# Output stores held until the next row's copy is stored, and the transposes of q and k moved in the DMA queue of an attention and MLP kernel

## The chip, the cores and the metric

The kernel runs on one core of a Trainium2 chip. The metric is the device time of one execution in microseconds (us); three runs of the kernel before gave 308.64, 310.31 and 312.22, so its median is 310.31. A core has five engines that run beside each other, each through its own queue of instructions in order: PE (matmuls), DVE (vector operations), ACT (activations and copies), POOL (casts, and the issue of some loads) and SP (the issue of the other DMA transfers). Which engine does what, and in which order, is written out by hand in this kernel; semaphores alone hold one engine back for another.

## What is computed

The reference is an attention with two kinds of masks, followed by a two-layer perceptron with a squared ReLU:

```python
# q, k, v: 8 batches, 8 heads, 576 positions, 64 wide
scores = scale * np.matmul(q, k.transpose(0, 1, 3, 2))
rel = pos[:, None] - pos[None, :]
mask_plain = (rel >= 0) & (rel < 32)                          # heads 0 to 3
mask_dil = (rel >= 0) & (rel < 32 * 4) & (rel % 4 == 0)       # heads 4 to 7
attn = softmax(where(mask, scores, -1e9))
y = np.matmul(attn, v)                # heads side by side: x is 4608 x 512
h = x @ w_in                          # 512 x 2048
g = np.maximum(h, 0.0) ** 2
out = g @ w_out                       # 2048 x 512, float32
```

## The kernel before, in words

**Two streams on PE.** The attention is done batch by batch; a "row" b is one batch, 0 to 7. The perceptron is done in nine blocks c of 512 tokens. Since 576 is more than 512, block c is complete once row c is, and in row b the kernel computes the attention of batch b while the matmuls of block b - 1 fill in between. The block is a Python generator (`moe_gen`), and `pump(n)` takes n steps of it; so the places of the `pump` calls in `attn_scores` and `attn_values` fix the order of PE's instructions. A step of the first layer (`mm1_gen`) is two matmuls, or four where the block's tokens lie on both sides of the end of the ring `xT`; 32 steps make its 16 groups. Each group is squared by ACT (`rt`, L321) and DVE (`g`, L322). From block 2 on, the second layer is a Strassen-like scheme (`mm2_strassen_gen`): DVE makes sums of quarters of g (L331, L332, L406, L418), PE accumulates products in the banks pa, pb and pc, and ACT copies pa out (`take`, L391) before PE adds the next product to the same bank.

**The attention of a row.** Scores are matmuls of the transposed q and k: `QKTp` for the sliding heads (ps, L573) and `QKTd` for the dilated ones (pz, L592). ACT takes the exponential (L563) and DVE multiplies by the mask (L564). The value products are pav (sliding, L622, three pairs of query blocks) and paw (dilated, L638, four). DVE normalises each (reciprocal L605, multiply L610). Then the result is transposed into `xT`: in rows 0 to 3 on PE (px L651, py L669) with a copy by ACT; from row 4 on by a DMA transpose on SP, straight into `xT` for the sliding heads (L680) and through a buffer yd for the dilated ones (L687), which ACT copies into `xT` (L675).

**How the next row is fetched.** From row 2 on, POOL first waits until the transposes into QKTd of this row have landed (`after_transposes`, L235), then loads sliding q and k of the next row (ns, L112) and copies the dilated ones inside DRAM (dd, L207). Somewhere in the row DVE brings ns into token order (nr, L120); SP stores that to DRAM (dp, L217), and later reads it back transposed into QKTp (L225), and dd into QKTd (L229). SP loads v as float32 (sv L132 for sliding, sd L137 for dilated heads); POOL casts it to vp (L169) and vd (L177). The last 32 keys of each query block of vp belong to the next block too, and 64 of vd: these "halos" are copied by ACT (L184, L189) in rows 0 to 2, and by DMA on SP (L194, L197) from row 3 on.

**What sets the order on SP.** SP carries out its list in order; an entry that has to wait (for data, for a buffer, or for the cast on POOL) holds everything behind it. In row 4 to 6 the list before is: vp halo and vd halo of the row; then, from hooks in `attn_values_by_dma`, dp (after the second pav), the two xT transposes, the first yd, sv, the second yd, two QKTp, two QKTd, and sd; then the two stores of the block's results (L397). In rows 2 and 3 one hook, `turn_and_load`, issues dp, sv, sd, two QKTp and two QKTd together. In row 2 it is called after the third pav, in row 3 after the last pz.

**The results.** Blocks 0 and 1 leave as rows of tokens (`store`), blocks 2 to 8 as two halves, ou and ov (`leave`), from a pool of three buffers tagged `ot`. Each store is issued on SP as soon as its half is named complete; only the second half of block 0 is held (`leave_first`).

The lines that the change and the prediction touch are `attn_scores` L692, `attn_values` L706, `attn_values_by_dma` L737, the driver loops L842 to L899, and the helpers named above. The halo rule of `attn_scores` and the hook of row 4 and later read:

```python
            if g and b < 3:
                halo_sliding(b, 0)
...
            av_sliding(b, mp, xs)
            if mp == 1:
                then[0]()
            pump(3)
```

Of the kernel before, what the change touches and what calls it, by code (L numbers as in the profile page):

```python
# [17 lines left out]
def kernel(  # L18
# [174 lines left out]
    def halo_sliding_by_dma(b):  # L193
        nc.sync.dma_start(out=vp[b % 2][0:PADP, 1:NB], in_=vp[b % 2][P - PADP : P, 0 : NB - 1])  # L194
# [29 lines left out]
        for i in (1, 0):  # L224
            nc.sync.dma_start_transpose(out=QKTp[b % 2][:, i, :, PADP:], in_=dp[i])  # L225

    def transpose_dilated(b, dd):
        for i in (1, 0):
            nc.sync.dma_start_transpose(out=QKTd[b % 2][:, i, :, KPAD:], in_=dd[i])  # L229


# [56 lines left out]
    for t, w in zip(wi, wi_cols):  # L288
        r = t.rearrange("p d (g f s) -> p d g f s", f=P, s=4)
        wi4 += [r[:, :, g] for g in range(w // 512)]  # L290

    def mm1_half(c, ffc, ph, dmks):
        lo = c * TOKC % XW
# [59 lines left out]
    def mm2_strassen_gen(c, g):  # L353
        A, Bk, Ck = "abc"
        banks = {}

        def wq(r, q):
            return lambda k: wo[2 * r + k // 4][:, k % 4, HM * q : HM * (q + 1)]

        def gq(i, r):  # L360
            return lambda k, t: g[:, HF * r + k, HTOK * i + P * t : HTOK * i + P * (t + 1)]

        def tq(n):
            return lambda k: wt[n][:, k]

        def sq(n):
            return lambda k, t: gs[n][:, k, P * t : P * (t + 1)]

        def product(bank, a, b, ts=(0, 1)):
            new = bank not in banks  # L370
            if new:
                banks[bank] = pmool.tile([P, 2, HM], FP32, name=f"p{bank}{c}", tag="pm")
            for t in ts:
                for k in range(HF):
                    nc.tensor.matmul(  # L375
                        banks[bank][:, t],
                        a(k, t),
                        b(k),
                        start=(new and t == 0 and k == 0),
                        stop=(k == HF - 1),  # L380
                        skip_group_check=True,
                    )
                    if k % 4 == 3 and (t, k) != (ts[-1], HF - 1):
                        yield

        def half(i):
            return otp.tile([P, 2, DM], FP32, name=f"o{i}_{c}", tag="ot")

        def take(o, j):
            ot = o[:, :, HM * j : HM * (j + 1)]  # L390
            nc.scalar.copy(ot, banks[A])  # L391
            return ot

        def leave(o, i, js):
            t0 = c * TOKC + HTOK * i
            m = slice(HM * js[0], HM * (js[-1] + 1))
            nc.sync.dma_start(  # L397
                out=out[t0 : t0 + HTOK, m].rearrange("(t p) m -> p t m", p=P), in_=o[:, :, m]
            )

        def add(ot, bank):
            nc.vector.tensor_add(ot, banks[bank], ot)  # L402

        last = c == NTOKC - 1

        nc.vector.tensor_sub(g[:, 0:HF, HTOK:], g[:, 0:HF, 0:HTOK], g[:, 0:HF, HTOK:])  # L406
        yield from product(A, gq(0, 0), wq(0, 0))
        upper = half("u")
        o11 = take(upper, 0)
        yield  # L410
        yield from product(Ck, gq(0, 1), wq(1, 0), (0,))
        yield
        yield from product(A, sq(1), tq(1))
        lower = half("v")
        o21 = take(lower, 0)
        yield
        yield from product(Bk, gq(1, 0), tq(2))
        nc.vector.tensor_sub(gs[1], g[:, HF:, 0:HTOK], gs[1])  # L418
        yield
        yield from product(A, sq(0), tq(0))  # L420
        o22 = take(lower, 1)
        add(o22, Bk)
        if last:
            leave(lower, 1, (1,))
        yield
        yield from product(Ck, gq(0, 1), wq(1, 0), (1,))
        add(o11, Ck)
        if last:
            leave(upper, 0, (0,))
        yield  # L430
        yield from product(A, sq(1), wq(1, 1))
        take(upper, 1)
        leave(upper, 0, (1,) if last else (0, 1))
        yield
        yield from product(Bk, gq(1, 1), tq(3))
        add(o21, Bk)
        leave(lower, 1, (0,) if last else (0, 1))
        yield
# [8 lines left out]
        )  # L447

    halves = {}
    first_out = []  # L450

    def leave_first():
        t, o = first_out.pop()
        nc.sync.dma_start(
            out=out[t * P : (t + 2) * P, :].rearrange("(t p) m -> p t m", p=P), in_=o
        )

    def store(c, t, po):
        if t % 2 == 0:
            halves[c] = otp.tile([P, 2, DM], FP32, name=f"ot{c}_{t}", tag="ot")  # L460
        ot = halves[c][:, t % 2]
        nc.scalar.copy(ot, po)
        if c:
            nc.sync.dma_start(out=out[(c * 4 + t) * P : (c * 4 + t + 1) * P, :], in_=ot)
        elif t % 2:
            first_out.append((t - 1, halves[c]))
            if t == 1:
                leave_first()

    def mm2_gen(c, g):  # L470
        for t in range(TOKC // P):
# [220 lines left out]
    def attn_scores(b, gap, less=0, hooks={}):  # L692
        for hp in range(2):
            s_sliding(b, hp)
            if hp in hooks:
                hooks[hp]()
            pump(gap)
        for g in range(2):
            s_dilated(b, g)
            if 2 + g in hooks:  # L700
                hooks[2 + g]()
            if g and b < 3:
                halo_sliding(b, 0)
            pump(gap - less)

    def attn_values(b, gap, wide=False, then=None):  # L706
        xs = x_tiles(b)
        for mp in range(3):
            av_sliding(b, mp, xs)
            if b < 3:  # L710
                if mp < 2:
                    halo_sliding(b, mp + 1)
                else:
                    halo_dilated(b, 0)
            if then and b == 2 and mp == 2:
                then()
            pump(gap)
        x_sliding(b, 0, xs, wide)
        if b < 3:
            halo_dilated(b, 2)  # L720
        pump(gap)
        av_dilated(b, 0, 0, xs)
        if then and b == 1:
            then()
        pump(gap)
        x_sliding(b, 1, xs, wide)
        pump(gap)
        av_dilated(b, 0, 1, xs)
        pump(gap)
        for a in range(2):  # L730
            av_dilated(b, 1, a, xs)
            pump(gap)
        x_dilated(b, 0, xs, wide)
        pump(gap)
        x_dilated(b, 1, xs, wide)

    def attn_values_by_dma(b, then):  # L737
        xs = x_tiles(b)
        for mp in range(3):
            av_sliding(b, mp, xs)  # L740
            if mp == 1:
                then[0]()
            pump(3)
        x_sliding_by_dma(b, xs)
        ys = []
        for t in range(2):
            for a in range(2):
                av_dilated(b, t, a, xs)
                pump(4 + 2 * (a > t))
            ys.append(x_dilated_by_dma(b, t, xs))  # L750
            then[1 + t](ys[t])
        pump(6)
        x_from(b, 0, ys[0])
        pump(7)
        x_from(b, 1, ys[1])
# [70 lines left out]
    for a in range(2):  # L826
        t_dilated(1, m, a, True)
        pump(2)
    attn_scores(1, 2, 1)
    dp = []  # L830
    attn_values(1, 1, True, lambda: dp.append(keep_sliding_qk(2, by_token(2, ns))))
    pump(1000)
    transpose_sliding(2, dp[0])
    transpose_dilated(2, dd)
    leave_first()
    load_v(2)


# [3 lines left out]
    for b in range(2, 4):  # L842
# [5 lines left out]
            cast_v(b)  # L848
        dd = keep_dilated_qk(nxt)
        if b == 3:  # L850
            halo_sliding_by_dma(b)
            halo_dilated_by_dma(b)

        def turn_and_load():
            dp = turn(nxt, ns)
            load_sliding_v(nxt)
            load_dilated_v(nxt, nc.sync)
            transpose_sliding(nxt, dp)
            transpose_dilated(nxt, dd)
            cast_v(nxt)  # L860

        pump(22 if b == 2 else 12)
        attn_scores(b, 4, 0, {3: turn_and_load} if b == 3 else {})
        attn_values(b, b, False, turn_and_load)
        pump(1000)

    for b in range(4, B):
        pending.append(moe_gen(b - 1))
        nxt = b + 1
        if nxt < B:  # L870
            after_transposes(b)
            ns = load_sliding_qk(nxt)
            dd = keep_dilated_qk(nxt)
        if b > 4:
            cast_dilated_v(b)
        halo_sliding_by_dma(b)
        halo_dilated_by_dma(b)
        dps = []

        def copied():  # L880
            if nxt < B:
                dps.append(turn(nxt, ns))

        def first(y):
            if nxt < B:
                load_sliding_v(nxt)

        def second(y):
            if nxt < B:
                transpose_sliding(nxt, dps[0])  # L890
                transpose_dilated(nxt, dd)
                load_dilated_v(nxt, nc.sync)
                nc.gpsimd.tensor_copy(seen, y[:, 0, 0, 0:1])
                cast_sliding_v(nxt)

        pump(3)
        attn_scores(b, 3)
        attn_values_by_dma(b, (copied, first, second))
        pump(1000)  # L899
    pending.append(moe_gen(B - 1))  # L900
    pending.append(moe_gen(B))
# [31 lines left out]
```

## Time and profile before

| what | value |
|---|---|
| median of three runs | 310.31 us |
| the profiled execution: its own time | 309.19 us |
| its span, first to last instruction | 307.1 us |
| granted TensorE clock | 1.00 |
| PE idle, 0 to 25 us / 25 to 277 us / 277 us to the end | 9.9 / 6.8 / 3.9 us |
| SP, DMA packets of its queue (q1) | 68832, 32.96 MB |
| POOL, DMA packets of its queue (q0) | 8752, 13.63 MB |
| longest waits of SP for an engine | 21.8 us (ov, L397), 22.5 us (ou, L397), 17.4 us (dp, L217) |

The profile is one execution on the chip, recorded by the hardware. A timeline line reads: start, length, engine, line of the code, operation, output<-input, and how many instructions are merged. A DMA line on SP or POOL is the time that the issue takes on that queue; the transfer lands later. A line of the waits reads: engine, line and tile that waited <- whom it waited for: total us, times, longest. Over the span, in 40 slices, the DMA engines were busy (in tenths) and moved GB/s:

```profile
DMA  7899998799599999995799979997983231003004
GB/s 116 187 204 213 208 173 152 157 215 221 119 211 176 242 191 187 258 187 120 127 171 260 220 126 188 267 189 131 158 252 22 45 111 40 2 1 139 0 1 138
```

### The profile page before, as it was taken

How to read it: one execution, taken by the hardware profiler on the slowest of the kernel's cores; microseconds unless marked ns; L12 is line 12 of the kernel's file. 1: busy time of each engine (PE TensorE's matmuls, PEld its weight loads, DVE VectorE, ACT ScalarE, POOL GpSimd, SP SyncE). 2: the span in 40 equal slices, each digit the busy share in tenths (PEclk: the TensorE clock that was granted, in tenths of full speed). 3: DMA queues.
4: the chain of work that ended last, by engine and by line, in shares of the span. 5: the costliest groups of instructions: out<-in, count | busy, mean ns of one | idle time of the engine just before them, and what ended most of it. 6: DMA issues, size and time to landing. Idle time of an engine off the chain costs nothing.

```text
span 307.1 us, 6899 instructions
## 1 busy us (share of the span) xinstructions
PE 286.5 (93%) x2762; PEld 192.4 (63%) x2762; DVE 210.1 (68%) x434; ACT 172.9 (56%) x293; POOL 64.2 (21%) x112
## 2 busy tenths in 40 slices
PE   1788998999999899999998999799989999999994
PEld 1345554555554468656887987458745875785584
DVE  7684447758843798489759984999398934834652
ACT  2766648668745863595457636763486446425620
POOL 4481027002704503310027002700230000000000
PEclk9999999999999999999999999999999999999999
DMA  7899998799599999995799979997983231003004
GB/s 116 187 204 213 208 173 152 157 215 221 119 211 176 242 191 187 258 187 120 127 171 260 220 126 188 267 189 131 158 252 22 45 111 40 2 1 139 0 1 138
DMA packets 77616, 47.03 MB, mean 153 GB/s; under 512 B 58480, under 2 KB 69232, under 8 KB 77584
## 3 DMA queue, kind: packets, MB, share of 16 engines
q1 hardware_dynamic: 68832, 32.96, 51.9%
q0 software_dynamic: 8752, 13.63, 26.1%
q8 instruction: 21, 0.34, 0.5%
q14 instruction: 11, 0.09, 0.1%
HBM read 36.70 MB, written 16.52 MB: 173 GB/s over the span
## 4 chain that ended last, share of the span: by engine, by line
PE 72%; DMA 12%; DVE 6%; SPq 3%; ACT 3%; issue 2%; POOL 0%; DVEq 0%; POOLq 0%
PE ph L298 32%; PE pa L375 15%; PE pb L375 7%; DMA vp<-vp 6%; PE po L441 6%; DMA QKTp<-dp 4%; PE pc L375 4%; PE paw L638 2%; PE pav L622 2%; DMA QKTd<-dd 1%; PE ps L573 1%; DMA sv<-in_v_dram 1%; ACT AT L563 1%; SPq L137 1%; SPq L132 1%
## 5 line engine op out<-in xcount | busy, mean ns | idle before, releaser
L298 PE MATMUL ph<-xT,wi 128*128 128x512 f16 (+1 forms) x640 | 134.2, 359 | 0.7 <-ACT xT L675 0.7
L321 ACT ACTIVATE rt<-ph 128x512 f16<-128x512 f32 x144 | 86.2, 608 | 47.5 <-PE ph L298 46.4
L298 PEld LDWEIGHTS <-wi 128*128 128x128 f16 x640 | 68.2, 114 | 45.9 <-issue 0.6
L322 DVE TENSOR_TENSOR g<-rt 128x512 f16<-128x512 f16 x144 | 63.4, 450 | 39.6 <-ACT rt L321 38.1
L375 PEld LDWEIGHTS <-g 128*128 128x128 f16 x448 | 43.3, 98 | 6.1
L375 PEld LDWEIGHTS <-gs 128*128 128x128 f16 x336 | 32.1, 98 | 4.0 <-DVE gs L332 0.3
L441 PE MATMUL po<-wo,g 128*128 128x512 f16 x128 | 33.1, 379 | 0.0
L402 DVE TENSOR_TENSOR ov<-pb,ov 128x512 f32<-128x512 f32 x14 | 9.7, 691 | 30.8 <-PE pb L375 17.4
L375 PE MATMUL pa<-wt,gs 128*128 128x256 f16 x224 | 27.2, 273 | 0.0
L375 PE MATMUL pb<-wt,g 128*128 128x256 f16 x224 | 27.1, 273 | 0.0
L169 POOL CAST vp<-sv 128x512 f16<-128x512 f32 x24 | 15.2, 664 | 53.4 <-DMA sv<-in_v_dram 39.5
L391 ACT COPY ov<-pa 128x512 f32<-128x512 f32 x14 | 8.2, 586 | 30.7 <-PE pa L375 30.7
L177 POOL CAST vd<-sd 128x512 f16<-128x512 f32 (+1 forms) x32 | 22.1, 717 | 11.4 <-PE ph L298 8.0
L610 DVE TENSOR_TENSOR xd<-paw,rcp_d 80x512 f16<-80x512 f32 (+1 forms) x32 | 21.9, 685 | 1.1
L563 ACT ACTIVATE AT<-pz 128x576 f16<-128x576 f32 x32 | 19.7, 694 | 1.2 <-PE pz L592 1.1
L563 ACT ACTIVATE AT<-ps 128x576 f16<-128x576 f32 x32 | 19.2, 657 | 2.2 <-PE ps L573 1.8
L564 DVE TENSOR_TENSOR AT<-AT,maskd 128x576 f16<-128x576 f16 x32 | 18.4, 604 | 1.8 <-ACT AT L563 0.7
L564 DVE TENSOR_TENSOR AT<-AT,maskp 128x576 f16<-128x576 f16 x32 | 15.5, 492 | 5.9 <-ACT AT L563 4.2
L391 ACT COPY ou<-pa 128x512 f32<-128x512 f32 x14 | 8.2, 586 | 15.8 <-PE pa L375 15.7
L610 DVE TENSOR_TENSOR xs<-pav,rcp_p 96x512 f16<-96x512 f32 x24 | 16.5, 687 | 0.8
L622 PEld LDWEIGHTS <-AT 128*128 128x128 f16 x192 | 9.3, 98 | 10.8 <-issue 6.0
L441 PEld LDWEIGHTS <-g 128*128 128x128 f16 x128 | 10.4, 98 | 8.3
(80 smaller groups left out, 276.7 us busy)
## 6 DMA issues: line engine op xcount, KB each, us to landing
sv<-in_v_dram SPq DMA_DIRECT2D x14, 288.0 KB, 5.3
dp<-nr SPq DMA_DIRECT2D x12, 288.0 KB, 4.0
out_dram<-ou SPq DMA_DIRECT2D x6, 512.0 KB, 4.0
out_dram<-ov SPq DMA_DIRECT2D x6, 512.0 KB, 4.7
sd<-in_v_dram SPq DMA_DIRECT2D x8, 320.0 KB, 6.2
ns<-in_k_dram POOLq DMA_DIRECT2D x8, 288.0 KB, 6.3
ns<-in_q_dram POOLq DMA_DIRECT2D x8, 288.0 KB, 7.8
sd<-in_v_dram SPq DMA_DIRECT2D x8, 256.0 KB, 6.0
```

The lines of the kernel that those rows point to most:

```text
L169: nc.gpsimd.tensor_copy(vp[b % 2][:, m : m + 2, :, 0:D], sv[:, :, m : m + 2, :].rearrange("p h m d -> p m h d"))
L177: nc.gpsimd.tensor_copy(vd[b % 2][p0:P, t, c : c + 2, :, 0:D], sd[p0:P, t, :, D * c : D * (c + 2)].rearrange("p h (c d) -> p c h d", d=D),)
L298: nc.tensor.matmul(ph[:, t0:t1], wi4[ffc // 4][:, dmk, :, ffc % 4], xT[:, dmk, x0 : x0 + t1 - t0], start=(dmk == 0 and t0 == 0), stop=(dmk ...
L321: nc.scalar.activation(rt, ph[:], ACTF.Relu)
L322: nc.vector.tensor_mul(g[:, ffc, :], rt, rt)
L375: nc.tensor.matmul(banks[bank][:, t], a(k, t), b(k), start=(new and t == 0 and k == 0), stop=(k == HF - 1), skip_group_check=True,)
L391: nc.scalar.copy(ot, banks[A])
L441: nc.tensor.matmul(po, g[:, ffc, t * P : (t + 1) * P], wo[ffc // 4][:, ffc % 4, :], start=(ffc == 0), stop=(ffc == NFF - 1),)
L563: nc.scalar.activation(AT[:, u, 0:UW], ps[:, :, 0 : UW // 2], ACTF.Exp, scale=scale)
L564: nc.vector.tensor_mul(AT[:, u, 0:UW], AT[:, u, 0:UW], mask)
L610: nc.vector.tensor_tensor(out=x, in0=pv, in1=rb, op=ALU.mult)
L622: nc.tensor.matmul(pav[:, i, h * (D + 2) : h * (D + 2) + D + 1], AT[:, 2 * (h // 2) + m // 3, off : off + P], vp[b % 2][:, m, h, 0 : D + 1 ...
```

## The change

The change makes five edits. (a) `leave_half` takes the place of the store calls; it puts the stores of blocks 2 to 4, and of the second halves of blocks 0 and 1, on a list, and `leave_held` issues the list. The two half-stores of block 1 (256 KB each) become one of 512 KB per pair. (b) In rows 2 and 3, `turn_and_load` runs after the second pav. It issues dp, the held stores, sv, two QKTp, one QKTd, the vp halo of the next row, the other QKTd, and sd; POOL casts sliding v there, and dilated v at the start of the next row. Row 3 pumps 14 steps ahead of the scores where it pumped 12. (c) From row 4 on, `copied` issues dp, the held stores, two QKTp and sv in one go: in row 4 after the second pav, in rows 5 and 6 after the last pz. (d) `loaded` follows the second yd transpose: it casts sliding v, then issues two QKTd, the vp halo of the next row, and sd. (e) In row 1 the first vp halo copy of ACT is put right after the second ps.

```diff
-    def transpose_dilated(b, dd):
-        for i in (1, 0):
+    def transpose_dilated(b, dd, sides=(1, 0)):
+        for i in sides:
             nc.sync.dma_start_transpose(out=QKTd[b % 2][:, i, :, KPAD:], in_=dd[i])
...
+    held = []
+
+    def leave_half(c, i, o, m, hold):
+        def go():
+            t0 = c * TOKC + HTOK * i
+            nc.sync.dma_start(
+                out=out[t0 : t0 + HTOK, m].rearrange("(t p) m -> p t m", p=P), in_=o[:, :, m]
+            )
+
+        if hold:
+            held.append(go)
+        else:
+            go()
+
+    def leave_held():
+        while held:
+            held.pop(0)()
...
         def leave(o, i, js):
...
+            leave_half(c, i, o, slice(HM * js[0], HM * (js[-1] + 1)), 1 < c < 5)
...
-        if c:
-            nc.sync.dma_start(out=out[(c * 4 + t) * P : (c * 4 + t + 1) * P, :], in_=ot)
-        elif t % 2:
-            first_out.append((t - 1, halves[c]))
-            if t == 1:
-                leave_first()
+        if t % 2:
+            leave_half(c, t // 2, halves[c], slice(0, DM), t > 1)
...
-            if g and b < 3:
+            if g and b == 2:
                 halo_sliding(b, 0)
...
-            if then and b == 2 and mp == 2:
+            if then and b > 1 and mp == 1:
                 then()
...
-    def attn_values_by_dma(b, then):
+    def attn_values_by_dma(b, copied, loaded):
...
-            if mp == 1:
-                then[0]()
+            if copied and mp == 1:
+                copied()
             pump(3)
...
             ys.append(x_dilated_by_dma(b, t, xs))
-            then[1 + t](ys[t])
+        loaded(ys[1])
         pump(6)
...
-    attn_scores(1, 2, 1)
+    attn_scores(1, 2, 1, {1: lambda: halo_sliding(1, 0)})
...
-    leave_first()
+    leave_held()
     load_v(2)
...
         if b == 3:
-            halo_sliding_by_dma(b)
+            cast_dilated_v(b)
             halo_dilated_by_dma(b)
 
         def turn_and_load():
             dp = turn(nxt, ns)
+            leave_held()
             load_sliding_v(nxt)
+            transpose_sliding(nxt, dp)
+            cast_sliding_v(nxt)
+            transpose_dilated(nxt, dd, (1,))
+            halo_sliding_by_dma(nxt)
+            transpose_dilated(nxt, dd, (0,))
             load_dilated_v(nxt, nc.sync)
-            transpose_sliding(nxt, dp)
-            transpose_dilated(nxt, dd)
-            cast_v(nxt)
-
-        pump(22 if b == 2 else 12)
-        attn_scores(b, 4, 0, {3: turn_and_load} if b == 3 else {})
+
+        pump(22 if b == 2 else 14)
+        attn_scores(b, 4)
         attn_values(b, b, False, turn_and_load)
...
-        if b > 4:
-            cast_dilated_v(b)
-        halo_sliding_by_dma(b)
+        cast_dilated_v(b)
         halo_dilated_by_dma(b)
-        dps = []
 
         def copied():
             if nxt < B:
-                dps.append(turn(nxt, ns))
+                dp = turn(nxt, ns)
+                leave_held()
+                transpose_sliding(nxt, dp)
+                load_sliding_v(nxt)
 
-        def first(y):
-            if nxt < B:
-                load_sliding_v(nxt)
-
-        def second(y):
+        def loaded(y):
             if nxt < B:
-                transpose_sliding(nxt, dps[0])
-                transpose_dilated(nxt, dd)
-                load_dilated_v(nxt, nc.sync)
                 nc.gpsimd.tensor_copy(seen, y[:, 0, 0, 0:1])
                 cast_sliding_v(nxt)
+                transpose_dilated(nxt, dd)
+                halo_sliding_by_dma(nxt)
+                load_dilated_v(nxt, nc.sync)
 
         pump(3)
-        attn_scores(b, 3)
-        attn_values_by_dma(b, (copied, first, second))
+        attn_scores(b, 3, 0, {3: copied} if b > 4 else {})
+        attn_values_by_dma(b, copied if b == 4 else None, loaded)
```

## The prediction

> **What bounds the kernel now.** I read first the busy times, then the waits of PE, then the timelines of the engines behind those waits. "Row b" is batch b, "MoE c" token block c.
>
> ```profile
> PE 286.5 (93%) x2762; PEld 192.4 (63%) x2762; DVE 210.1 (68%) x434; ACT 172.9 (56%) x293; POOL 64.2 (21%) x112
> ```
> PE is the bound: 307.1 of span less 286.5 leaves 20.6 us idle. By stages, 9.9 of it lie before 25 us and 3.8 after 277, where the change has nothing. The change adds or removes no matmul, so it can only move waits. In PE's waits these two are its targets (total, times, longest):
> ```profile
> PE pav L622 <- DMA vp<-vp: 3.8, 3, 1.6
> PE ps L573 <- DMA QKTp<-dp: 1.0, 1, 1.0
> ```
> The first falls in rows 5, 6 and 7 (at 165.8, 197.2 and 228.9 us). SP's timeline for row 5 says why:
> ```profile
> 151.89 2.65 SPq L225 DMA_TRANSPOSE QKTp<-dp  x2
> 154.64 4.24 SPq L229 DMA_TRANSPOSE QKTd<-dd  x2
> 158.93 1.37 SPq L137 DMA_DIRECT2D sd<-in_v_dram  x2
> 160.41 0.54 SPq L397 DMA_DIRECT2D out_dram<-ou  x1
> 161.04 0.42 SPq L397 DMA_DIRECT2D out_dram<-ov  x1
> 161.55 0.72 SPq L194 DMA_DIRECT2D vp<-vp  x1
> ```
> The halo copy vp<-vp (its source was cast by 155.35 on POOL) stands behind loads and two stores, and lands 5.53 us after issue, with PE waiting. In row 3 QKTp likewise stood behind sv and sd (issues 85.84 to 92.4) and landed at 100.86.
>
> Two places have room for a new wait. In row 3 DVE was busy 8.70 of 8.90 us from 108.3 to 117.2; its end:
> ```profile
> 113.55 0.69 DVE L610 TENSOR_TENSOR xs<-pav,rcp_p 96x512 f16<-96x512 f32 x1
> 114.16 0.41 DVE L322 TENSOR_TENSOR g<-rt 128x512 f16<-128x512 f16 x1
> 114.61 0.69 DVE L331 TENSOR_TENSOR gs<-g 128x1024 f16<-128x1024 f16 x1
> 115.33 0.69 DVE L332 TENSOR_TENSOR gs<-gs,g 128x1024 f16<-128x1024 f16 x1
> 115.94 1.22 DVE L406 TENSOR_TENSOR g<-g 128x2048 f16<-128x2048 f16 x1
> ```
> And row 4 on SP, ACT and PE, in that order:
> ```profile
> 140.03 1.14 SPq L217 DMA_DIRECT2D dp<-nr  x2
> 141.25 3.78 SPq L680 DMA_TRANSPOSE xT<-xs  x2
> 145.66 1.81 SPq L687 DMA_TRANSPOSE yd<-xd  x1
> ...
> 149.99 1.30 ACT L675 COPY xT<-yd 128x640 f16<-128x640 f16 x1
> 152.88 0.59 ACT L391 COPY ov<-pa 128x512 f32<-128x512 f32 x1 [1.58 <-PE pa L375]
> ...
> 153.55 1.91 PE L375 MATMUL pa<-wo,gs 128*128 128x256 f16 x16
> ```
> ACT reads yd at 149.99, then copies bank A out (L391); PE writes that bank again at 153.55. So yd may land at 153.55 - 0.59 - 1.30 = 151.7 at the latest.
>
> **What the Trainium skill says.** "DMA: Bandwidth & Descriptors", Anatomy of one DMA: semaphore waits happen on the issuing sequencer, before dispatch; so a waiting transfer holds all behind it on SP. The trace agrees (the halo above). Same page, "Two DMAs through the same engine are not ordered": a read of what an earlier DMA wrote must wait for its completion. So QKTp<-dp waits for dp's landing, 3.7 us after issue in row 4. Same page, "Issuing engines are not separate DMA queues": SP's and POOL's transfers share 16 engines; sv landed in 4.5 us in row 4, 8.4 beside dd in row 2. "SBUF — State Buffer", "SBUF: two separate sides": DVE and GpSimd lock a shared port pair. The trace agrees in size: a mask multiply takes 0.45 us, but 0.82 beside the POOL cast at 165.8.
>
> **What is gained.** In rows 5 to 7 the halo follows QKTd directly, ahead of sd and the stores: row 5's about 4 us earlier, landing in time: -3.8. In row 3 QKTp no longer stands behind sd (3.31 us of issue), and two more MoE chunks (0.87 us, `pump(14)`) come before the scores: -1.0. In row 1 the ACT halo copy (0.41) moves ahead of the exponentials; PE waited 0.55 for it, and the exponentials give back 0.41: -0.15. Sum -4.95.
>
> **What is paid.**
> (1) Row 3, DVE. With 14 chunks ahead, 30 instead of 28 are out before the first value product; so the L322, L331, L332 and L406 shown above (ending 117.16) now precede the second normalise (L610, ended 114.24) on DVE. It then ends at 117.16, less `nr` (0.75, now behind it), less 0.1 to 0.2 of earlier start: 116.3; the dilated casts, moved beside it on POOL, add about 0.3: 116.6. The PE transpose px, at 114.78 before, stands behind 0.87 more work and comes 1.02 + 0.2 sooner: 114.4. PE waits 2.2 (0.8 if DVE's idle time earlier in the row is used, 3.0 if POOL collides more).
> (2) `nr` for row 4 then ends at about 117.3, not 111.6. dp lands 3.9 later (121.3), the QKTp pair takes 2.7 to 5.3 of SP and lands about 6 later: 128 to 130, against PE at 128.66 - 1.15 + 2.2 = 129.7. The last QKTd, behind v's cast and the halo, lands near 132, against 133.3. Taken as 0, at most 1.
> (3) Row 4, SP. The hook stays at the same place, but ahead of xT there are now two held stores (0.5 each, inside the wait for dp), the QKTp pair and sv. From the same start: 140.03 + 3.7 for dp, + 2.65 for the pair, + 1.2 for sv, + 3.3 for the xT pair (row 5's), + 3.2 for yd to land = 154.1; less 151.7: PE waits 2.4. With every step at its shortest (xT 2.5) 1.6; with the pair at row 3's 5.3 it is 5.
> (4) Rows 5 and 6. The hook comes right behind the last dilated scores, about 2.85 us earlier (mask multiply ended 136.4 in row 4, `nr` began 139.25). That pays for (3) with 0.4 to spare. But ns for the next row is fetched only after QKTd has landed and takes 7.4 to 8.9; DVE may stand at `nr` for it. I take 0.4 each, 0.8 in sum (0 to 3).
> (5) At nothing: sd behind the transposes and its casts a row later (sd lands near 108 and 135, casts 2.4 to 3.2, first paw at 116.5 and 140.3; without that 2 us of cover in row 4, the excess is paid 1 to 1); vd's halo (wanted at 145.2); the stores, two 256 KB made one of 512, held one row: of three `ot` buffers the one of u2 is wanted again at 149.4, and lands near 147. A landing after that holds ACT by as much; this is the tightest of these covers. Row 7 loads nothing.
>
> Sum: -4.95 + 2.2 + 2.4 + 0.8 = +0.45. The profiled execution took 309.19 (span 307.1); that gives 309.6. It stood 1.12 below the median of 310.31; so I forecast **310.8**. About 1%, 3.1 us, is what a measurement can tell from no change.
>
> **Rivals.**
> *The gains stay.* For it: the waits removed are real, and the halo is the last thing PE waits for in three rows. If (1) and (3) come out at their shortest and (4) at nothing: -4.95 + 0.8 + 1.6 = -2.55, median 307.8; if they don't show at all, 305.4. Against it: (3) follows from SP's order alone.
> *Slower: the transposes of QKTp clog SP.* The pair took 2.65 to 2.87 us of SP in rows 4 to 6, where no load went just ahead, but 5.65 and 5.29 in rows 2 and 3, behind sv and sd. Now 1 MB of stores goes just ahead in rows 4 to 6. If the pair then takes 5.3, yd is 2.6 later in each: 2.6 more in row 4, 2.2 in each of rows 5 and 6 beyond their 0.4 of room: +0.45 + 7.0 - 0.8 = +6.65, median 317.0. It decides from a pair of about 3.1 us in rows 5 and 6. Against it: the stores move in 2 to 5 us, most of which the wait for dp covers.
> *It doesn't do what it says*: excluded for the order, as it is written out by hand; in rows 2 and 3 sv still precedes the transposes.
>
> **Chances.** Forecast case (-2 to +3.5) 0.52; gains stay 0.18; clogged queue 0.30. Faster by over 1% needs nearly all gains kept: 0.14. Slower by over 1%: most of the clogged case and the upper edge of the forecast: 0.35. Within: 0.51. The range, 306.5 to 316, reaches into both.
>
> **What would show it.** Right: no wait of pav on vp<-vp in rows 5 to 7, none of ps on QKTp in row 3; new waits of px on DVE's xs in row 3 and, in row 4, of L375 on ACT's copy behind "xT <- DMA yd". Wrong: ACT not waiting for yd in row 4 (then faster), or ACT waiting over 2 us for yd in rows 5 and 6 (then slower).

## The result, and the profile after

The kernel after took 320.82 us (median of four executions, 318.12 to 322.07), the one before 310.39 beside it: a ratio of 1.0324, with a 95% interval of 1.0235 to 1.0413. It is slower by 3.2%, where 310.8 had been forecast with a range up to 316.0. The profiled execution is the fastest of the four: 318.12, with a span of 316.1; before, those were 309.19 and 307.1. So the trace has 9.0 us of span to explain, of the 10.4 between the medians.

The busy times first, as before:

```profile
PE 288.8 (91%) x2762; PEld 193.5 (61%) x2762; DVE 208.9 (66%) x434; ACT 172.7 (55%) x293; POOL 62.8 (20%) x112
```

PE has the same 2762 matmuls and stands idle 27.3 us instead of 20.6. It is also busy for 2.3 us more with the same work, which needs an explanation of its own. Then PE's waits (total, times, longest):

```profile
PE pa L393 <- ACT ov L409: 8.6, 3, 4.8
...
PE px L654 <- DVE xs L613: 1.8, 1, 1.8
PE ps L576 <- DMA QKTp<-dp: 0.7, 1, 0.7
```

The two waits that the change aimed at are gone or smaller: no wait on the vp halo is left in rows 5 to 7 (3.8 before), and of the wait on QKTp, 1.0 in row 3 before, 0.7 stands in row 4 now. But the second layer's bank (L393, before L375) waits three times for ACT's copy of it (L409, before L391), once each in rows 4, 5 and 6. In PE's waits before there is none of them.

SP in row 4, in the order of its issues:

```profile
142.92 1.42 SPq L217 DMA_DIRECT2D dp<-nr  x2
144.46 0.52 SPq L297 DMA_DIRECT2D out_dram<-ou  x1
145.03 1.49 SPq L297 DMA_DIRECT2D out_dram<-ov  x1
146.63 5.50 SPq L225 DMA_TRANSPOSE QKTp<-dp  x2
152.19 1.21 SPq L132 DMA_DIRECT2D sv<-in_v_dram  x2
153.44 3.12 SPq L683 DMA_TRANSPOSE xT<-xs  x2
156.66 2.53 SPq L690 DMA_TRANSPOSE yd<-xd  x2
```

Before, the QKTp pair took 2.65 us of SP here; behind the two held stores (1 MB together) it takes 5.50, and all that follows is late by the difference. In rows 5 and 6 it takes 4.26 and 4.96 (before: 2.87 and 2.65):

```profile
179.84 4.26 SPq L225 DMA_TRANSPOSE QKTp<-dp  x2
...
211.65 4.96 SPq L225 DMA_TRANSPOSE QKTp<-dp  x2
```

ACT is the next link: it reaches its copy of yd (L678) and stands there for 6.77 us, with the copy of bank A behind it in its queue:

```profile
159.58 1.26 ACT L678 COPY xT<-yd 128x640 f16<-128x640 f16 x1 [6.77 <-DMA yd<-xd]
160.75 0.58 ACT L409 COPY ov<-pa 128x512 f32<-128x512 f32 x1
```

PE's timeline then shows what that costs, in rows 4, 5 and 6 (start, length, and in brackets the idle time before it):

```profile
161.38 3.27 PE L393 MATMUL pa<-wo,gs 128*128 128x256 f16 x16 [4.82 <-ACT ov L409]
...
194.58 1.91 PE L393 MATMUL pa<-wo,gs 128*128 128x256 f16 x16 [1.75 <-ACT ov L409]
...
226.54 1.91 PE L393 MATMUL pa<-wo,gs 128*128 128x256 f16 x16 [2.02 <-ACT ov L409]
```

The same 16 matmuls take 3.27 us after the idle 4.82 and 1.91 after the shorter ones. The table by stretches of row 4 (length; PE busy and matmuls; granted clock; share of the DMA engines; GB/s) says why:

```profile
core 0: us, PE busy (x), PEclk, DMA share, GB/s
...
152.00:156.00 4.00, 4.00 (x39) 1.00 1.20 249
156.00:161.00 5.00, 0.56 (x6) 0.98 0.84 140
161.00:164.00 3.00, 2.62 (x13) 0.50 0.98 183
164.00:166.20 2.20, 2.20 (x21) 0.95 0.79 204
```

After the pause the granted clock is 0.50 for 3.4 us (from 160.8 to 164.2), which costs about 1.4 on the 16 matmuls (3.27 less 1.91): part of the 2.3 us that PE is busier. Where the rest lies is open. The Trainium skill, "TensorE: Matmul & The Clock Gate", section "Part 1: The HAM clock gate", says that the clock is halved after an idle window of about 3.4 us and restored after as long a busy one. The 3.4 us at 0.50 are of that length, and PE had stood idle since 156.6 when the clock fell. But PE was back at work only 2.8 us before the clock was restored, and other kernels told below halve the clock after a shorter pause or after none (last section). The mean clock of this execution was 0.992, of the three longer ones 0.981, 0.981 and 0.989. That these lost more to the clock would fit the 2.7 us between the profiled run and the median, but it is not shown: the mean also counts the end of the span, where PE is done and a halved clock costs nothing (here from 314.3 on), and where the others lost it is not known.

By rows, from the first matmul of the first layer (ph) in a row to that of the next, from PE's timelines (us; the last four are experiments told below):

| kernel | row 3 | row 4 | row 5 | row 6 | row 7 |
|---|---|---|---|---|---|
| before | 32.73 | 29.77 | 31.40 | 31.56 | 31.00 |
| after | 32.94 | 37.57 | 31.84 | 31.96 | 29.78 |
| after, no stores of blocks 2 to 4 | 33.14 | 34.34 | 30.02 | 29.78 | 29.77 |
| before, early halo | 31.65 | 29.78 | 32.29 | 31.19 | 29.83 |
| the same, rows 2 and 3 changed | 32.95 | 32.65 | 33.08 | 30.90 | 29.81 |
| before, early halo, nr later | 33.91 | 30.16 | 30.95 | 30.30 | 29.83 |

29.77 is a row from 4 on without a wait. Row 4 alone loses 7.8 us; rows 5 and 6 gain the halo, give it back and lose 0.4 more each, and only row 7 keeps its gain of 1.2.

### The profile page after: what moved, and what is told of

It reads as the page before. It is cut to its first block, busy times and chain, and to the rows that moved or that the text cites. A ratio compares the mean times of both kernels' runs of the same rounds, so it can differ in the third digit from the quotient of the medians.

```text
span 316.1 us, 6877 instructions
## 1 busy us (share of the span) xinstructions
PE 288.8 (91%) x2762; PEld 193.5 (61%) x2762; DVE 208.9 (66%) x434; ACT 172.7 (55%) x293; POOL 62.8 (20%) x112
## 4 chain that ended last, share of the span: by engine, by line
PE 62%; DVE 19%; ACT 8%; DMA 6%; issue 3%; SPq 1%; POOL 0%; DVEq 0%; POOLq 0%
PE ph L316 28%; PE pa L393 10%; PE po L455 8%; PE pb L393 6%; DVE g L340 4%; ACT AT L566 3%; DMA yd<-xd 3%; DVE xd L613 3%; DVE AT L567 2%; DMA ns<-in_q_dram 2%; DVE xs L613 2%; PE pc L393 2%; ACT rt L339 2%; DVE gs L349 2%; DVE gs L350 2%
## 5 line engine op out<-in xcount | busy, mean ns | idle before, releaser
L340 DVE TENSOR_TENSOR g<-rt 128x512 f16<-128x512 f16 x144 | 63.8, 455 | 38.8 <-ACT rt L339 38.0
L393 PEld LDWEIGHTS <-g 128*128 128x128 f16 x448 | 43.2, 98 | 6.0
L393 PEld LDWEIGHTS <-gs 128*128 128x128 f16 x336 | 33.0, 100 | 14.1 <-issue 9.1
L393 PE MATMUL pa<-wt,gs 128*128 128x256 f16 x224 | 27.2, 273 | 0.3 <-DVE gs L350 0.3
L393 PE MATMUL pb<-wt,g 128*128 128x256 f16 x224 | 27.1, 273 | 0.0
L169 POOL CAST vp<-sv 128x512 f16<-128x512 f32 x24 | 14.4, 632 | 61.0 <-DMA sv<-in_v_dram 57.1
L393 PE MATMUL pa<-wo,gs 128*128 128x256 f16 x112 | 14.9, 289 | 8.6 <-ACT ov L409 8.6
L409 ACT COPY ov<-pa 128x512 f32<-128x512 f32 x14 | 8.2, 585 | 23.7 <-PE pa L393 23.7
L567 DVE TENSOR_TENSOR AT<-AT,maskp 128x576 f16<-128x576 f16 x32 | 17.5, 567 | 5.1 <-ACT AT L566 4.0
L409 ACT COPY ou<-pa 128x512 f32<-128x512 f32 x14 | 8.2, 586 | 19.8 <-PE pa L393 19.6
L678 ACT COPY xT<-yd 128x640 f16<-128x640 f16 (+1 forms) x8 | 9.5, 1189 | 15.2 <-DMA yd<-xd 15.2
L567 DVE TENSOR_TENSOR AT<-AT,maskd 128x576 f16<-128x576 f16 x32 | 15.9, 527 | 1.4 <-ACT AT L566 0.6
```

The lines of the kernel that those rows point to most:

```text
L169: nc.gpsimd.tensor_copy(vp[b % 2][:, m : m + 2, :, 0:D], sv[:, :, m : m + 2, :].rearrange("p h m d -> p m h d"))
L340: nc.vector.tensor_mul(g[:, ffc, :], rt, rt)
L393: nc.tensor.matmul(banks[bank][:, t], a(k, t), b(k), start=(new and t == 0 and k == 0), stop=(k == HF - 1), skip_group_check=True,)
L567: nc.vector.tensor_mul(AT[:, u, 0:UW], AT[:, u, 0:UW], mask)
```

## The experiments

**Theory:** the pair of QKTp transposes is slow on SP because 1 MB of stores goes just ahead of it, and yd is late by that. **Rival 1:** it is the order alone (QKTp and sv ahead of xT). **Rival 2:** row 4 starts with damage from row 3 (the new place of the hook, 14 steps), and what is seen on SP only follows.

### Stores not held (after, ratio 1.0168)

```diff
-            leave_half(c, i, o, slice(HM * js[0], HM * (js[-1] + 1)), 1 < c < 5)
+            leave_half(c, i, o, slice(HM * js[0], HM * (js[-1] + 1)), False)
```

> The changed kernel, but the stores of blocks 2 to 4 leave when complete, as before; nothing but dp stands ahead of the QKTp pair in rows 4 to 6. Theory clog (the held stores stretch the pair's issue on SP from 2.7 to 4.3-5.5 us): the pair takes 2.6 to 3.0, PE's wait for ACT's copy of pa falls from 8.6 to about 2.5 in sum (row 4 alone), 313 to 315 us. Theory order (the pair and sv ahead of the result's transposes are enough, stores or not): the pair still takes over 4, the wait stays at 7 to 9, 319 to 321 us.

Measured: 314.60 us, ratio 1.0168 (1.0106 to 1.0230). SP and DVE of this kernel in row 4:

```profile
144.75 1.13 SPq L217 DMA_DIRECT2D dp<-nr  x2
148.02 2.74 SPq L225 DMA_TRANSPOSE QKTp<-dp  x2
```

```profile
143.96 0.76 DVE L120 COPY nr<-ns 128x2304 f16<-128x2304 f16 x1 [2.14 <-DMA ns<-in_q_dram]
```

The pair is back at 2.74 (2.68 and 2.73 in the next rows), and PE waits for ACT's copy once, 2.4 us, instead of 8.6 in three. So the stores ahead do stretch the pair. But row 4 is no shorter (38.88): the stores now run beside the load of ns, whose second half lands 9.3 us after its issue instead of 5.2 in the kernel after, and DVE, in order, stands at nr for it; PE then waits 1.9 for a normalise behind nr.

### No stores of blocks 2 to 4 (after, ratio 1.0057)

This kernel never writes the results of token blocks 2, 3 and 4; all else is done as in the kernel after.

```diff
-            leave_half(c, i, o, slice(HM * js[0], HM * (js[-1] + 1)), 1 < c < 5)
+            if not 1 < c < 5:
+                leave_half(c, i, o, slice(HM * js[0], HM * (js[-1] + 1)), False)
```

> The changed kernel with the stores of blocks 2 to 4 left out (those rows of the result are not written), so that the order on SP stands alone: the QKTp pair and sv ahead of xT and yd, no store ahead of them and none beside ns. If order and clog both count: the pair takes 2.6 to 2.9, ns comes early, PE still waits 2 to 3 us for ACT's copy of pa in row 4 and under 0.5 in rows 5 and 6; 311 to 313 us. If the clog was all: no wait in any row, 308 to 309 us. If the order was all: waits as in the changed kernel, 8 us or more, 318 us or more.

Measured: 311.27 us, ratio 1.0057 (1.0029 to 1.0085). Its SP and its PE in row 4:

```profile
146.27 2.81 SPq L225 DMA_TRANSPOSE QKTp<-dp  x2
149.13 1.81 SPq L132 DMA_DIRECT2D sv<-in_v_dram  x2
151.04 3.03 SPq L684 DMA_TRANSPOSE xT<-xs  x2
```

```profile
158.85 1.91 PE L393 MATMUL pa<-wo,gs 128*128 128x256 f16 x16 [2.36 <-ACT ov L409]
```

This is the order without the stores, and it separates theory from rival 1: the order costs 2.36 in row 4, and no such wait is left in rows 5 and 6. With the stores ahead the waits are 4.82, 1.75 and 2.02, and the halved clock follows the first of them; it does not show in the profiled execution here. Between this kernel and the kernel after lie 2.7% of the time before.

### QKTp behind yd (after, ratio 1.0058)

```diff
                 leave_held()
-                transpose_sliding(nxt, dp)
+                dps.append(dp)
+
+        def first():
+            if nxt < B:
                 load_sliding_v(nxt)
...
+                transpose_sliding(nxt, dps[0])
                 nc.gpsimd.tensor_copy(seen, y[:, 0, 0, 0:1])
```

> The changed kernel, but from row 4 on the QKTp pair stands behind the second yd transpose and sv behind the first, as before; dp and the held stores stay ahead of xT. Theory order: yd lands in time, PE's wait for ACT's copy of pa is under 1 us in sum, the slow first product of row 4 goes with it, 309 to 311 us. Theory clog: the stores stretch the xT pair instead (5 us for 3.1 to 4.3), 1 to 3 us of the wait stay, 311 to 314 us.

Measured: 311.60 us, ratio 1.0058 (1.0015 to 1.0102). Stores ahead of xT, QKTp from row 4 on where it was before: no wait of PE for ACT's copy is left at all. Next behind the stores stands the xT pair, here in row 4:

```profile
143.81 0.52 SPq L297 DMA_DIRECT2D out_dram<-ou  x1
144.38 1.52 SPq L297 DMA_DIRECT2D out_dram<-ov  x1
145.99 5.05 SPq L683 DMA_TRANSPOSE xT<-xs  x2
151.15 1.22 SPq L690 DMA_TRANSPOSE yd<-xd  x1
```

In row 4 the stretch falls on xT (5.05, before 3.78); in rows 5 and 6 it takes 3.80 and 4.25, against 3.32 and 4.26 before. So the xT pair, too, can be stretched behind the stores, but here its delay did not reach PE through ACT. The wait came out as expected of the order, the time as expected of the clog. The rest of the loss is elsewhere: px in row 3 (1.8), QKTp late in row 5 (1.6) and nr standing for ns in row 5 (2.38 us of DVE, then pav waits 2.5).

### 12 steps in row 3 (after, ratio 1.0250)

```diff
-        pump(22 if b == 2 else 14)
+        pump(22 if b == 2 else 12)
```

> The changed kernel with 12 steps ahead of row 3's scores again, not 14. If DVE's order made the wait of px (1.8 us): it goes, nr comes some 2 to 4 us earlier, QKTp's wait in row 4 (0.7) goes too, while ps may wait up to 0.9 for QKTp of row 3: 318 to 320 us. If the wait had another cause (casts beside DVE), px still waits over 1 us and the time stays at 320 to 321.

Measured: 317.01 us, ratio 1.0250 (1.0191 to 1.0309). That is below the 318 to 320 expected. The waits of px and of QKTp are gone, and dp of row 4 is issued at 140.39 instead of 142.92, but PE is earlier by as much, and the wait in row 4 is the same:

```profile
PE pa L393 <- ACT ov L409: 8.4, 3, 5.0
```

That is against rival 2: row 4's loss does not come from row 3. The ratio is 0.0074 lower than the kernel after's, 2.3 us, which is the size of the two waits removed (1.8 and 0.7), though the intervals overlap.

### Early halo alone (before, ratio 0.9937)

```diff
-        halo_sliding_by_dma(b)
+        else:
+            halo_sliding_by_dma(b)
...
                 transpose_sliding(nxt, dps[0])
-                transpose_dilated(nxt, dd)
-                load_dilated_v(nxt, nc.sync)
                 nc.gpsimd.tensor_copy(seen, y[:, 0, 0, 0:1])
                 cast_sliding_v(nxt)
+                transpose_dilated(nxt, dd)
+                halo_sliding_by_dma(nxt)
+                load_dilated_v(nxt, nc.sync)
```

> The kernel before with one part of the change alone: in rows 4 to 6 the next row's vp halo and sd follow QKTd, the halo first, ahead of the stores. If the halo wait was all that PE lost there: no wait of pav on vp, 306 to 307 us (3.8 less than before). If another transfer was as late (QKTd, or sd's cast): the wait moves to pz or paw, 309 to 311 us.

Measured: 307.79 us, ratio 0.9937 (0.9904 to 0.9970). The halo's 3.8 us of waits are gone; 0.63% of the time, some 2 us, is gained, about half of what was expected if the halo was all. DVE in row 5 shows what is next:

```profile
171.88 0.76 DVE L120 COPY nr<-ns 128x2304 f16<-128x2304 f16 x1 [1.51 <-DMA ns<-in_q_dram]
```

With the halo no longer late, PE and DVE come to the second pav sooner, and ns, which lands 9.6 us after its issue beside the stores, is late for nr; PE waits 1.2 us for the normalise behind it.

### Early halo, and rows 2 and 3 as in the kernel after (ratio 1.0050)

```diff
-            if then and b == 2 and mp == 2:
+            if then and b > 1 and mp == 1:
...
         if b == 3:
-            halo_sliding_by_dma(b)
+            cast_dilated_v(b)
             halo_dilated_by_dma(b)
...
-            load_dilated_v(nxt, nc.sync)
             transpose_sliding(nxt, dp)
-            transpose_dilated(nxt, dd)
-            cast_v(nxt)
+            cast_sliding_v(nxt)
+            transpose_dilated(nxt, dd, (1,))
+            halo_sliding_by_dma(nxt)
+            transpose_dilated(nxt, dd, (0,))
+            load_dilated_v(nxt, nc.sync)
 
-        pump(22 if b == 2 else 12)
-        attn_scores(b, 4, 0, {3: turn_and_load} if b == 3 else {})
+        pump(22 if b == 2 else 14)
+        attn_scores(b, 4)
...
-        if b > 4:
-            cast_dilated_v(b)
-        else:
-            halo_sliding_by_dma(b)
+        cast_dilated_v(b)
```

> The kernel before with the early halo, and with rows 2 and 3 as in the changed kernel (hook after the second pav, 14 steps ahead of row 3's scores, dilated v cast a row later); stores not held, rows 4 to 6 as before but for the halo and the cast. If rows 2 and 3 cost on their own: the wait of px (1.8 us) and a late nr in row 4 show, and it is 1 to 3 us slower than the early halo alone (0.9937): 1.000 to 1.005. If they are free: 0.99 to 0.995.

Measured: 311.11 us, ratio 1.0050 (1.0022 to 1.0079), about 3.5 us more than without these edits. PE's waits:

```profile
PE paw L638 <- DVE xs L610: 3.1, 2, 1.5
PE px L651 <- DVE xs L610: 2.0, 2, 1.8
```

px is the wait forecast for row 3. The paw waits are in rows 4 and 5: nr stands for ns there (1.77 and 2.14 us of DVE). So the edit of rows 2 and 3 costs by itself, with the stores not held.

### Stores held until dp, with the early halo (ratio 0.9965)

```diff
+            if 1 < c < 5:
+                held.append(go)
+            else:
+                go()
...
                 dps.append(turn(nxt, ns))
+                leave_held()
```

> The kernel before with the early halo, and the stores of blocks 2 to 4 held until dp of the next row is issued, ahead of xT. If stores beside ns made DVE stand at nr in the early-halo kernel: ns lands in 5 to 7 us instead of up to 9.6, that wait (1.5 us in row 5) goes, xT's pair takes 4 to 5 us but yd is still in time: 0.983 to 0.990. If the stores only move the trouble: ACT or QKTp waits 1 us or more, 0.993 or worse.

Measured: 308.73 us, ratio 0.9965 (0.9936 to 0.9995). The stores no longer run beside ns, and DVE no longer stands at nr; but the xT pair behind the stores takes 4.30, 5.28 and 4.29 us in rows 4 to 6, and QKTp comes late in four rows, 2.5 us in all. Against 0.9937 there is no gain, and the intervals overlap.

### Early halo, and nr behind the first paw (ratio 0.9905)

```diff
             av_sliding(b, mp, xs)
-            if mp == 1:
-                then[0]()
             pump(3)
...
                 av_dilated(b, t, a, xs)
+                if t == a == 0:
+                    then[0]()
```

> The kernel before with the early halo, and with nr and dp one value product later, behind the first paw and the xT transposes. If DVE standing at nr for ns was what kept the early halo from its 3.8 us: no wait of paw on DVE, 0.985 to 0.990. If dp then comes too late for QKTp: a wait of ps on QKTp, 0.994 or worse.

Measured: 307.16 us, ratio 0.9905 (0.9872 to 0.9938), faster than both kernels and just short of the 0.985 to 0.990 expected. Its interval overlaps that of the early halo alone (0.9904 to 0.9970). DVE no longer stands at nr; the longest wait left behind the start is in row 3, where nothing was changed:

```profile
PE ps L573 <- DMA QKTp<-dp: 2.2, 1, 2.2
```

### The same, with sd behind the transposes in row 2 (ratio 0.9908)

```diff
         if b == 3:
+            cast_dilated_v(b)
             halo_sliding_by_dma(b)
...
             load_sliding_v(nxt)
-            load_dilated_v(nxt, nc.sync)
+            if b == 3:
+                load_dilated_v(nxt, nc.sync)
             transpose_sliding(nxt, dp)
             transpose_dilated(nxt, dd)
-            cast_v(nxt)
+            if b == 2:
+                load_dilated_v(nxt, nc.sync)
+                cast_sliding_v(nxt)
+            else:
+                cast_v(nxt)
```

> The kernel is the one with nr behind the first paw (ratio 0.9905), and in row 2 alone sd is issued behind the QKTp and QKTd transposes, with the casts of dilated v at the start of row 3. If the order in row 2 is good by itself and the loss of the changed rows 2 and 3 came from the earlier place of the hook and the 14 steps in row 3, then the wait of ps on QKTp in row 3 (2.2 us) is gone, no px wait on DVE's xs appears, and the ratio is 0.984 to 0.989. If the order of sd itself costs (its casts and the vd halo late in row 3, dp behind that halo on SP), the wait comes back on paw or on row 4's QKTp and the ratio is 0.990 to 0.998.

Measured: 306.18 us, ratio 0.9908 (0.9878 to 0.9938), beside a kernel before of 308.68 in that session. In its waits the line above reads:

```profile
PE ps L573 <- DMA QKTp<-dp: 0.3, 1, 0.3
```

The wait in row 3 is gone (the 0.3 is in row 5) and none came in its place, as the first reading expected. But the ratio is that of the kernel without this edit: it lies in the range of the second reading, whose waits don't show, though 0.988 to 0.989 lies within its interval. The wait that was removed varies from one execution to the next: with row 3 untouched it was 1.0 before, 2.2 in the kernel above, and none in the early halo alone (row 3: 32.73, 33.91, 31.65). So 2.2 overstated it; what the edit is worth on average, these runs can't tell.

## Why the prediction was wrong

**The step that failed is (3), row 4 on SP, in one term of its sum: "+ 2.65 for the pair".** It measured 5.50. The other terms held: dp to the pair 3.71 (3.7 forecast), sv 1.25 with its gap (1.2), xT 3.22 (3.3), yd from its issue to ACT's copy 2.92 (3.2). From the row's first matmul, yd was forecast at 26.8 (154.1 less the row's start at 127.27) and came at 30.9: 2.85 from the pair, 1.5 from a dp later in the row, less 0.3 elsewhere. PE itself reached the bank 1.6 later in the row, which cancels the dp; so the wait was 4.8 and not 2.4. With no stores ahead the pair took 2.81 and the wait 2.36, the forecast's number. That it agrees so closely is in part luck: there sv took 1.9 where 1.2 was forecast and three other terms were 0.2 to 0.3 shorter, and dp came 2.1 later in the row, as PE did at the bank. The duration had been taken from the row of the same tile, though its neighbour on the queue was to change; the text named that as a rival.

**Step (4), rows 5 and 6:** 0.4 each was forecast, for ns standing late; 1.75 and 2.02 came, and from the pair again (4.26 and 4.96). Without the stores nothing was left there. That nr may stand for ns was a real danger, but it shows where the stores are not held.

**The clock was left out.** A pause of PE was priced at its length. After the 4.82 us in row 4 came about 1.4 more at clock 0.50.

**The gains were nearly as forecast.** Halo: 3.8 gained in the waits. QKTp in row 3: the 1.0 went, and 0.7 came back in row 4, where step (2) had 0, at most 1. In row 1 the wait of 0.55 for ACT's halo copy went, but PE then waited 0.70 for a reciprocal of DVE (L608) in the same row: where -0.15 was forecast, +0.15 shows in the waits. At the start of the kernel the loads of ns made PE wait 1.8 us longer than before, with nothing of the change ahead of them.

**Step (1), row 3 on DVE,** came out by its mechanism and nearly its size. DVE's timeline of the kernel after, end of that stretch (L340 to L420 were L322 to L406):

```profile
113.50 0.41 DVE L340 TENSOR_TENSOR g<-rt 128x512 f16<-128x512 f16 x1
113.95 0.70 DVE L349 TENSOR_TENSOR gs<-g 128x1024 f16<-128x1024 f16 x1
114.68 0.69 DVE L350 TENSOR_TENSOR gs<-gs,g 128x1024 f16<-128x1024 f16 x1
115.29 1.22 DVE L420 TENSOR_TENSOR g<-g 128x2048 f16<-128x2048 f16 x1
116.42 0.20 DVE L608 RECIPROCAL rcp_p<-pav 96x8 f32<-96x8 f32 x1
116.65 0.69 DVE L613 TENSOR_TENSOR xs<-pav,rcp_p 96x512 f16<-96x512 f32 x1
```

The four are ahead of the second normalise, which ends at 117.3 (116.6 forecast); px waited 1.8 (2.2 forecast).

**The sum:** -3.8 (halo), -0.3 (QKTp), +1.3 (px: 1.8 in row 3, while one of 0.5 in row 0 is gone), +8.6 (bank A), +2.3 (PE busier), +0.6 (start: +1.8 for ns, -1.2 for one wait on ACT) make 8.7 of the 9.0 us. Forecast for the same: +0.45.

**The rivals.** The one in which the transposes clog SP had the mechanism and said 317.0; it decided from a pair of 3.1 us. What it left out is in the main PE's busier time (2.3), of which the clock explains about 1.4. Its argument against itself, that the wait for dp covers the stores, fell: 3.71 us lay between dp and the pair, but of the 7.7 us from the first store's issue to the last one's landing they covered 2.2, and the stores landed 4.9 to 7.1 us after their issue where it had 2 to 5. It was given 0.30 and should have been the forecast, since rows 2 and 3 of the same profile showed a pair behind large transfers at 5.65 and 5.29, and row 1, which the prediction did not read, showed one just behind a held store of 512 KB:

```profile
60.01 0.43 SPq L454 DMA_DIRECT2D out_dram<-ot  x1
60.86 4.08 SPq L225 DMA_TRANSPOSE QKTp<-dp  x2
```

No row showed a pair fast behind a large load or store issued just ahead of it.

**One reading was off.** The halo of row 5 was taken to show that a waiting transfer holds all behind it. It stood behind long issues: SP issued from 151.89 to 161.55 with hardly a pause. An entry that waits shows in the kernel without stores: SP stands from 144.30 to 146.27 for dp, with sv, xT and yd behind it.

## What to carry to other kernels

Take the time of a transfer's issue from a row with the same neighbours on the queue, not from the same line in another place: the QKTp pair behind 1 MB of stores held SP up to twice as long. Where an in-order queue is the thing that is late, moving a store away from one victim gives it the next (nr beside it, xT or QKTp behind it). Here moving the waiting work, nr behind the first paw, did better than moving the stores (0.9905 against 0.9965, both with the early halo; the intervals just touch). And a long pause of PE can cost more than its length: both pauses of near 5 us in row 4 were followed by some 1.4 us of loss to the clock.

## What was not expected of the hardware

The stretch of a transpose's issue: from row 4 on, 2.64 to 3.05 us for the QKTp pair without a load of v or a store of results directly ahead of it on SP, 4.26 to 5.50 with 1 MB of stores in the kernel after. There the issue of the pair ended when the last held store landed, in all three rows: at 152.13, 184.10 and 216.61, with ov's landing at 152.1, 184.1 and 216.6 (its issue plus 7.1, 6.0 and 6.7). The traces show more of this than these three. In rows 1, 2 and 3 of the kernel before, the pair ended at 64.94, 98.15 and 122.78, and the last transfer ahead of it on SP (the held store, then sd twice) landed at 64.8, 98.1 and 122.8. So the profile before already held the pattern by which the pair of the kernel after could have been timed. Over all eleven kernels, 39 pairs have a load of v or a store of results directly ahead of them on SP, and each ended within 0.4 us of that landing.

This points to an issue that gets through only as the transfers ahead drain. It is not proven by it: where xT stood behind the stores, its issue ended up to 0.9 us before that landing (row 6 of the kernel with the early halo and held stores: 210.44 and 211.3). Nor is it a matter of transposes alone: the second store of a block (ov) took 1.49 to 1.66 us to issue in rows 4 to 6 of the kernel after, right behind dp and the first, and 0.41 to 0.42 in the one before. No kernel here issued the stores from another engine's queue, so whether the place in SP's queue counts, or only that the stores are under way, stays open.

The second half of ns took 5.2 to 5.7 us to land in row 4 of three kernels without stores just ahead of it (the kernel after, no stores, QKTp behind yd), and 9.3 and 9.6 in two where the stores left just before (stores not held; rows 2 and 3 changed).

The clock: 0.50 followed pauses of 4.8 and 5.0 us, and one of 2.44 in the kernel with stores not held; pauses of 1.75, 2.02, 2.36 and even 2.52 (QKTp behind yd) showed no dip. So the length of the single pause does not decide by itself. Nor does a dip need a pause: in two kernels (12 steps in row 3, early halo alone) the clock fell to 0.50 between 25 and 26 us, where PE had not stood idle for more than 0.7 us at a time since 15 us, and the 60 first-layer matmuls there took 14.80 us instead of 13.11. Each of the five dips seen before PE's last matmul lasted about 3.4 us.
